# Two of the first weight loads of a recurrence-and-maxout kernel issued on the ScalarE queue instead of the SyncE queue

## The chip, the cores and the metric

The kernel runs on one core of a Trainium2 chip. The metric is the device time of one execution in microseconds.

The profile's span is counted from the first to the last instruction and is about 1.8 us shorter than the time of the same run.

## The reference, cut to what matters

```python
sig = 1 / (1 + exp(-f_logit));  f = lb + (1 - lb) * sig;  i = 1 - f
for t in range(S):                       # S = 6144, 4 sequences, 256 channels
    h = f[:, t] * h + i[:, t] * x[:, t]
    y[:, t] = h
h1 = y @ w1;  h2 = y @ w2                # 24576 tokens, 256 -> 1024
out = maximum(h1, h2) @ w_out            # 1024 -> 256
```

The kernel uses max(h1, h2) = h1 + relu(h2 - h1). It needs the difference w2 - w1, scaled and rounded to bf16 (`wd`), and the product w1 @ w_out (`w13` in the code, not to be confused with the load of the same name).

## The kernel before

The tokens are worked on in 48 blocks of 512. The weights and the first four blocks come in by 26 loads, nearly all of 256 KB, all on the SyncE queue and in this order:

```python
LOADS = """
f0a x0a f0b w13 w23 x0b w12 w22 wo3 w10 w20 w11 wo2 w21 f1a x1a wo0 f1b x1b wo1
f2a f2b x2a x2b f3 x3
"""
```

Here `f0a` is the first half of block 0 of `f_logit`, `x0b` the second half of block 0 of `x`, `w13` quarter 3 of w1, `w23` quarter 3 of w2, `wo3` quarter 3 of w_out. The names appear in the profile without their numbers: `fn`, `xn`, `w1n`, `w2n`, `won`.

A list says in which order each engine gets the small steps of the start. Its beginning:

```python
PLAN = """
G0a RW3.p keeps_T keeps V0a TU0a D31.p warm3 TV0a D30.p G0b F0a0.v warm4 TU0b
D21.p F0a1.v S0a1 S0a0 V0b F0b1.a warm1 TW3 F0b0.a RW0.p warm5 TV0b RW2.v S0b1
D01.p KW3.a TW2 SC31.a SC30.a KW2.a S0b0 RO3.a H06a H07a D20.v SC21.a warm3 H06b
SC20.v H07b D00.v W133 RW1.v R07.a TW0 H04b H04a ...
"""
```

The letter behind the point is the engine: v VectorE, a ScalarE, p GpSimd.
- `G` is the gate, a sigmoid of `f` on ScalarE; `V` is gate times `x` on VectorE (`vn` in the profile); `TU`, `TV` turn them on TensorE; `F` and `S` are the decay and the scan, with `y` as the result.
- `RW2` rounds quarter 2 of w1 (`w1b`); `D21`, `D20` subtract w1 from w2 (`wdf`), one half of a quarter each; `SC` scales the difference (`wd`).
- `H06b` and the like are the hidden matmuls `dT<-y,wd`; `warm` are matmuls that only keep TensorE busy. **H04b** is the ninth hidden matmul. From it on TensorE runs with hardly a gap, so its start is used below as the end of the start-up.

From block 4 on the tokens come another way. GpSimd issues a DMA that casts them to bf16 in DRAM (`cast`), and SyncE issues DMA transposes (`fT`, `xT`). The first cast waits for `x2b`, by a one-column copy into `held`.

```python
def load(j, s, half=None):
    ...
    nc.sync.dma_start(out=ins[j][s][:, q0:q1, :], in_=...)
...
nc.scalar.dma_start(out=lbr[:], ...)      # the lower bound, 1 KB
for name in LOADS.split():
    load_item(name)
```

Of the kernel before, what the change touches and what calls it, by code (L numbers as in the profile page):

```python
# [16 lines left out]
def kernel(  # L17
# [13 lines left out]
    nc = tc.nc  # L31
# [50 lines left out]
    w13 = wpool.tile([P, KC, D], BF16)  # L82
# [4 lines left out]
    def alloc_in(j):  # L87
        fn = inpool.tile([P, NQ, D], FP32, name="fn")
        xn = inpool.tile([P, NQ, D], FP32, name="xn")
        ins[j] = (fn, xn)  # L90
        us[j] = natpool.tile([P, NQ, D], BF16, name="un")
        vs[j] = natpool.tile([P, NQ, D], BF16, name="vn")
        ffs[j] = nffpool.tile([P, KC, TB], BF16, name="nff")
        ys[j] = ypool.tile([P, KC, TB], BF16, name="y")

    def load(j, s, half=None):

        src = (f_logit, x)[s]
        q0, q1 = (0, NQ) if half is None else (2 * half, 2 * half + 2)
        nc.sync.dma_start(  # L100
            out=ins[j][s][:, q0:q1, :],
            in_=src[0, j * TB + q0 * P : j * TB + q1 * P, :].rearrange(
                "(q p) d -> p q d", p=P
            ),
        )
# [70 lines left out]
    def turn_dma(c):  # L176
        for s, name in enumerate(("fs", "xs")):
            t = ttpool.tile([P, KC, CB * TB], BF16, name=("fT", "xT")[s])
            turned[c, s] = t
            nc.sync.dma_start_transpose(out=t[:], in_=spare[c % NS, name][:])  # L180

    def cast_behind(c):

        if c + 1 < NCH:
            last = CB * TB - 1
            nc.gpsimd.tensor_copy(out=held[:], in_=turned[c, 0][:, KC - 1, last : last + 1])  # L186
            cast(c + 1)
# [5 lines left out]
    def gate(j):  # L193
        ffs[j] = midpool.tile([P, KC, TB], BF16, name="ff")
        ys[j] = ypool.tile([P, KC, TB], BF16, name="y")
        us[j] = midpool.tile([P, KC, TB], BF16, name="u")
        nc.scalar.activation(out=us[j][:], in_=part(j, 0), func=AF.Sigmoid, scale=-1.0)  # L197

    def drive(j):
        vs[j] = midpool.tile([P, KC, TB], BF16, name="v")  # L200
        nc.vector.tensor_tensor(out=vs[j][:], in0=us[j][:], in1=part(j, 1), op=ALU.mult)  # L201

    def forget_half(j, h, on_act=False):
        forget(ffs[j][:, h, :], us[j][:, h, :], h, on_act)

    def scan_half(j, h):
        scan(j, h, 0, TB, vs[j][:, h, :])
# [45 lines left out]
    def hidden(j, fc):  # L253
        hidden_whole(j, fc)
        relu(j, fc)
# [49 lines left out]
    def project(j, slot):  # L305
        i, half_ = divmod(slot, 2)
        n = FC + KC
        project_steps(j, i, half_ * n // 2, (half_ + 1) * n // 2)
# [17 lines left out]
    def store(j, g):  # L326
        copy_out(j, g)
        send_out(j, g)

    def store_row(j, g, r):  # L330
        osb = lastpool.tile([P, D], FP32, name="row")
        nc.vector.tensor_copy(out=osb[:], in_=pos[j, g, r][:, 0, :])  # L332
        r0 = j * TB + 2 * g * P
        nc.sync.dma_start(
            out=out[r0 : r0 + 2 * P, :].rearrange("(p r) d -> p r d", r=2)[:, r, :],
            in_=osb[:],
        )
# [1 line left out]

    QF = DFF // 4  # L340

    def weight_load(k, w, src):
        cols = slice(k * QF, (k + 1) * QF)
        nc.sync.dma_start(  # L344
            out=w[:, :, cols], in_=src[:, cols].rearrange("(h p) f -> p h f", p=P)
        )

    def wout_load(k):
        nc.sync.dma_start(
            out=won[:, 2 * k : 2 * k + 2, :],  # L350
            in_=moe_w_out[k * QF : (k + 1) * QF, :].rearrange("(q p) c -> p q c", p=P),
        )
# [78 lines left out]
    def keep_warm(n):  # L431
        for _ in range(n):
            nc.tensor.matmul(  # L433
                idle[:].rearrange("p r d -> p (r d)"),
                lhsT=warm[:, 0:P],
                rhs=warm[:],
                start=True,
                stop=True,
            )
# [26 lines left out]

    engines = {"a": nc.scalar, "v": nc.vector, "p": nc.gpsimd}

    def load_item(name):
        if name[:2] == "wo":  # L470
            wout_load(int(name[2]))
        elif name[0] == "w":
            w, src = ((w1n, moe_w1), (w2n, moe_w2))[int(name[1]) - 1]
            weight_load(int(name[2]), w, src)
        else:
            half = ("ab".index(name[2]),) if len(name) == 3 else ()
            load(int(name[1]), "fx".index(name[0]), *half)

    outs = []

# [70 lines left out]
    with tc.manual_schedule():  # L551
        for j in range(NP):
            alloc_in(j)
        nc.scalar.dma_start(out=lbr[:], in_=lower_bound.rearrange("(h p) -> h p", p=P))
        for name in LOADS.split():
            load_item(name)
        nc.vector.memset(warm[:], 0.0)  # L557
        make_identity(nc, ident[:])
        nc.vector.tensor_copy(out=ident_b[:], in_=ident[:])
        keep_warm(7)  # L560
        for item in PLAN.split():
            issue(item)
        assert not outs

        for j in range(3, NBLK + 1):
            for fc in range(FC):
                if j < NBLK:
                    hidden(j, fc)
                project(j - 1, fc)
                if fc == 0 and j > 3:  # L570
                    store(j - 2, 1)
                if fc == 4 and j < NBLK:
                    store(j - 1, 0)
                if j == NBLK and fc in (3, 5, 7):
                    if fc == 3:
                        store(j - 1, 0)
                    else:
                        store_row(j - 1, 1, (fc - 5) // 2)
                if (j, fc) in gate_of:
                    b = gate_of[j, fc]  # L580
                    gate(b)
                    drive(b)
                    for h in range(KC):
                        forget_half(b, h)
                        scan_half(b, h)
                if (j, fc) in turn_of:
                    turn_dma(turn_of[j, fc])
                    cast_behind(turn_of[j, fc])
# [30 lines left out]
```

## Time and profile before

| | kernel before |
|---|---|
| median of 3 runs | 397.38 us (397.21 to 397.8) |
| TensorE busy | 387.6 of 395.6 us |
| DMA that the start waits for last, by the chain | x0b, issued 3.29, landed 8.71 us |
| H04b starts | 13.45 us |

First the page of the kernel before: span, busy time with its share and the number of instructions, and the chain that ended last, by engine.

```profile
span 395.6 us, 7146 instructions
## 1 busy us (share of the span) xinstructions
PE 387.6 (98%) x2793; PEld 275.0 (70%) x2840; DVE 251.2 (63%) x366; ACT 273.3 (69%) x451; POOL 39.2 (10%) x83
...
## 4 chain that ended last, share of the span: by engine, by line
PE 95%; DMA 1%; DVE 1%; issue 1%; SPq 1%; DVEq 0%
...
```

TensorE is busy nearly everywhere, and it makes 95% of the chain. What is left is the start. The stages of one microsecond show it; the columns are as the head line says, and the last two are the mean share of the 16 DMA engines (it can pass 1 where packets overlap) and what they moved.

```profile
...
core 0: us, PE busy (x) PEld busy (x) DVE busy (x) ACT busy (x) POOL busy (x), PEclk, DMA share, GB/s
2.00:3.00 1.00, 1.00 (x4) 0.43 (x3) 0.00 (x0) 0.60 (x1) 0.00 (x0) 1.00 0.86 241
3.00:4.00 1.00, 1.00 (x4) 0.18 (x2) 0.00 (x0) 0.38 (x1) 0.00 (x0) 1.00 0.99 327
4.00:5.00 1.00, 1.00 (x7) 0.70 (x7) 0.41 (x3) 0.25 (x1) 0.00 (x0) 1.00 0.88 296
5.00:6.00 1.00, 1.00 (x4) 0.34 (x3) 0.94 (x3) 0.00 (x0) 0.00 (x0) 1.00 1.04 331
6.00:7.00 1.00, 1.00 (x8) 0.52 (x7) 0.42 (x1) 0.63 (x1) 0.14 (x1) 1.00 0.83 284
9.00:10.00 1.00, 0.15 (x1) 0.00 (x0) 1.00 (x2) 0.90 (x2) 0.46 (x1) 1.00 1.06 361
...
```

From 9 us on the loads come at about 350 GB/s, before that a little slower. Then the timeline of VectorE from x0b's landing (start, duration, engine, line, operation, names; in brackets the idle time before it and what ended that):

```profile
...
start us, us, engine line op out<-in xcount [idle before <-releaser]
8.80 1.20 DVE L113 TENSOR_TENSOR vn<-un,xn 128x512 bf16<-128x512 bf16 x1 [0.96 <-DMA xn<-in_x_dram]
9.93 0.41 DVE L355 CAST w1b<-w1n 128x512 bf16<-128x512 f32 x1
10.56 1.38 DVE L149 TENSOR_TENSOR_SCAN y<-nff,y,dT 128x256 bf16<-128x256 bf16 x2 [0.21 <-issue]
11.86 0.79 DVE L380 TENSOR_TENSOR wdf<-w2n,w1n 128x256 f32<-128x256 f32 x1
12.68 0.72 DVE L388 TENSOR_SCALAR wd<-wdf,om 128x256 bf16<-128x256 f32 x1
...
```

and of TensorE, GpSimd and ScalarE in the same stretch:

```profile
...
10.06 0.40 PE L126 MATMUL dT<-ident_b,vn 128*128 128x128 bf16 x4 [0.91 <-DVE vn L113]
...
13.45 0.72 PE L225 MATMUL dT<-y,wd 128*128 128x256 bf16 x5 [0.20 <-DVE wd L388]
```

```profile
...
8.05 1.41 POOL L380 TENSOR_TENSOR wdf<-w2n,w1n 128x256 f32<-128x256 f32 x2 [0.58 <-DMA w2n<-in_moe_w_dram]
...
```

```profile
...
1.32 1.28 ACT L108 ACT_TABLE_LOAD   x1 [1.32 <-PEq L603]
3.62 0.63 ACT L108 ACTIVATE un<-fn 128x512 bf16<-128x512 f32 x1 [1.02 <-DMA fn<-in_f_logit_dram]
6.11 0.63 ACT L108 ACTIVATE un<-fn 128x512 bf16<-128x512 f32 x1 [1.86 <-DMA fn<-in_f_logit_dram]
...
```

VectorE works without a real pause from 8.80 to 13.40, and TensorE's matmul at 13.45 has waited 0.20 us for its last `wd`. In the chain of waits this reads as "x0b, then VectorE, then TensorE". The `vn` at 8.80 took 1.20 us; the one at 4.73 took 0.68, as most do.

### The profile page before, as it was taken

To read this page: it belongs to the slowest core of one execution; us is meant where nothing else is said; L and a number is where in the kernel's file an instruction comes from. 1 tells how busy PE (TensorE), PEld (TensorE's weight loads), DVE (VectorE), ACT (ScalarE), POOL (GpSimd) and SP (SyncE) were. 2 spreads that over 40 slices of the span, in tenths; PEclk is the share of its full clock that TensorE was granted. 3 is DMA by queue.
4 is the path that set the end of the run, shared out by engine and by line. 5 is a ranking of instruction groups with operands and counts; after the bars stand their busy time and mean duration, and the time that the engine had idled before them with its cause. 6 is when DMAs were issued, how large, how long until landed. Compare 5 with 4: busy or idle time off the path is not lost.

```text
span 395.6 us, 7146 instructions
## 1 busy us (share of the span) xinstructions
PE 387.6 (98%) x2793; PEld 275.0 (70%) x2840; DVE 251.2 (63%) x366; ACT 273.3 (69%) x451; POOL 39.2 (10%) x83
## 2 busy tenths in 40 slices
PE   8999999999999999999999999999999999999996
PEld 3796777676667777767677777666677777676775
DVE  4896965756755775576567656755775576567622
ACT  4787676677667666766676677667766766676661
POOL 2511011011101101001011011011011010100000
PEclk9999999999999999999999999999999999999999
DMA  7989999999999999999999999999898898981122
GB/s 252 350 220 211 211 206 216 216 221 225 200 228 201 203 230 178 229 220 202 199 232 209 188 228 191 195 208 230 198 204 213 186 202 193 217 188 55 53 81 107
DMA packets 125078, 79.12 MB, mean 200 GB/s; under 512 B 94194, under 2 KB 101620, under 8 KB 125044
## 3 DMA queue, kind: packets, MB, share of 16 engines
q1 hardware_dynamic: 113072, 55.59, 59.8%
q0 software_dynamic: 11968, 23.07, 35.7%
q8 instruction: 22, 0.36, 0.4%
q14 instruction: 12, 0.10, 0.1%
q10 hardware_dynamic: 4, 0.00, 0.0%
HBM read 53.48 MB, written 48.23 MB: 257 GB/s over the span
## 4 chain that ended last, share of the span: by engine, by line
PE 95%; DMA 1%; DVE 1%; issue 1%; SPq 1%; DVEq 0%
PE psO L268 53%; PE dT L245 39%; PE dT L225 2%; DMA xn<-in_x_dram 1%; PE dT L126 1%; SPq L100 0%; PE psO L413 0%; DVE vn L113 0%; SPq L344 0%; DVE y L149 0%; DVE wd L388 0%; DVE wdf L380 0%; DVE row L332 0%; PE dT L396 0%; DVEq L113 0%
## 5 line engine op out<-in xcount | busy, mean ns | idle before, releaser
L240 ACT ACTIVATE rt<-dT 128x512 bf16<-128x512 f32 x382 | 222.9, 596 | 104.4 <-PE dT L245 101.2
L268 PE MATMUL psO<-wob,rt 128*128 128x256 bf16 x1536 | 231.0, 273 | 0.2
L268 PEld LDWEIGHTS <-rt 128*128 128x128 bf16 x1536 | 150.0, 98 | 94.7 <-issue 0.2
L245 PE MATMUL dT<-y,wd 128*128 128x512 bf16 x690 | 208.8, 379 | 2.2
L149 DVE TENSOR_TENSOR_SCAN y<-ff,y,v 128x512 bf16<-128x512 bf16 x82 | 105.2, 1283 | 2.9
L317 DVE COPY osb<-psO 128x512 f32<-128x512 f32 x93 | 62.6, 678 | 65.6 <-PE psO L268 65.6
L245 PEld LDWEIGHTS <-wd 128*128 128x128 bf16 x736 | 72.0, 98 | 8.8
L268 PE MATMUL psO<-w,y 128*128 128x256 bf16 x384 | 72.4, 273 | 0.0
L201 DVE TENSOR_TENSOR v<-u,xT 128x1024 bf16<-128x1024 bf16 x44 | 30.4, 691 | 62.7 <-ACT u L197 50.8
L197 ACT ACTIVATE u<-fT 128x1024 bf16<-128x1024 bf16 x44 | 46.1, 1049 | 3.1 <-DMA fT<-fs 3.1
L268 PEld LDWEIGHTS <-y 128*128 128x128 bf16 x384 | 37.6, 98 | 4.4
L186 POOL CAST held<-fT 128x1 f32<-128x1 bf16 x21 | 6.7, 319 | 278.9 <-DMA fT<-fs 278.9
L138 DVE TENSOR_SCALAR ff<-u,nom 128x512 bf16<-128x512 bf16 x88 | 29.7, 338 | 0.0
L170 POOL DMA_DIRECT2D fs<-in_f_logit_dram x22 | 12.3, 558 | 4.3 <-issue 4.3
L170 POOL DMA_DIRECT2D xs<-in_x_dram x22 | 12.1, 549 | 0.0
L149 DVE TENSOR_TENSOR_SCAN y<-nff,y,dT 128x256 bf16<-128x256 bf16 x14 | 9.6, 731 | 1.8 <-PE dT L126 1.5
L225 PE MATMUL dT<-y,wd 128*128 128x256 bf16 x64 | 10.1, 273 | 0.3 <-DVE wd L388 0.2
L433 PE MATMUL psO<-warm 128*128 128x512 bf16 x22 | 7.8, 492 | 1.2 <-DVE warm L557 1.2
L149 DVE TENSOR_TENSOR_SCAN y<-ff,v 128x512 bf16<-128x512 bf16 x6 | 7.4, 1225 | 0.2
L108 ACT ACTIVATE un<-fn 128x512 bf16<-128x512 f32 x8 | 5.0, 628 | 3.3 <-DMA fn<-in_f_logit_dram 3.0
L225 PEld LDWEIGHTS <-wd 128*128 128x128 bf16 x64 | 5.8, 98 | 1.4 <-issue 0.4
L113 DVE TENSOR_TENSOR vn<-un,xn 128x512 bf16<-128x512 bf16 x8 | 6.1, 767 | 1.0 <-DMA xn<-in_x_dram 1.0
(40 smaller groups left out, 52.2 us busy)
## 6 DMA issues: line engine op xcount, KB each, us to landing
out_dram<-osb SPq DMA_DIRECT2D x95, 256.0 KB, 3.4
fs<-in_f_logit_dram POOLq DMA_DIRECT2D x22, 512.0 KB, 6.8
xs<-in_x_dram POOLq DMA_DIRECT2D x22, 512.0 KB, 9.6
fn<-in_f_logit_dram SPq DMA_DIRECT2D x6, 256.0 KB, 6.0
xn<-in_x_dram SPq DMA_DIRECT2D x6, 256.0 KB, 5.7
w1n<-in_moe_w_dram SPq DMA_DIRECT2D x4, 256.0 KB, 5.9
w2n<-in_moe_w_dram SPq DMA_DIRECT2D x4, 256.0 KB, 6.0
won<-in_moe_w_out_dram SPq DMA_DIRECT2D x4, 256.0 KB, 6.0
```

The source lines that it names most:

```text
L138: nc.vector.tensor_scalar(out=o, in0=i, scalar1=nom[:, h : h + 1], scalar2=1.0, op0=ALU.mult, op1=ALU.add)
L149: nc.vector.tensor_tensor_scan(out=ys[j][:, h, t0:t1], data0=ffs[j][:, h, t0:t1], data1=v, initial=initial, op0=ALU.mult, op1=ALU.add,)
L170: nc.gpsimd.dma_start(out=spare[c % NS, name][:], in_=src[b, k * TB : (k + CB) * TB, :], max_dma_last_dim=4096,)
L186: nc.gpsimd.tensor_copy(out=held[:], in_=turned[c, 0][:, KC - 1, last : last + 1])
L197: nc.scalar.activation(out=us[j][:], in_=part(j, 0), func=AF.Sigmoid, scale=-1.0)
L201: nc.vector.tensor_tensor(out=vs[j][:], in0=us[j][:], in1=part(j, 1), op=ALU.mult)
L225: nc.tensor.matmul(dts[j, fc][:, tok], lhsT=wd[:, kc, unit(fc)], rhs=ys[j][:, kc, tok], start=(first and kc == 0), stop=(not first and kc ...
L240: nc.scalar.activation(out=rt[:], in_=dts[j, fc][:], func=AF.Relu)
L245: nc.tensor.matmul(dts[j, fc][:], lhsT=wd[:, kc, unit(fc)], rhs=ys[j][:, kc, :], start=(kc == 0), stop=(kc == KC - 1),)
L268: nc.tensor.matmul(ps, lhsT=lhsT, rhs=rhs, start=start, stop=stop, skip_group_check=True)
L317: nc.vector.tensor_copy(out=osbs[j, g][:], in_=pos[j, g, 0][:])
L433: nc.tensor.matmul(idle[:].rearrange("p r d -> p (r d)"), lhsT=warm[:, 0:P], rhs=warm[:], start=True, stop=True,)
```

## The change

The intent: SyncE needs 0.51 us for each issue, so the sixth load goes out only at 3.29. ScalarE has a queue too, and until its first gate at 3.62 it only issues one small load and loads a table (1.32 to 2.60). Two weight loads are issued there, beside the token loads.

```diff
-    def load(j, s, half=None):
+    def load(j, s, half=None, eng=nc.sync):
...
-    def weight_load(k, w, src):
+    def weight_load(k, w, src, eng=nc.sync):
         cols = slice(k * QF, (k + 1) * QF)
-        nc.sync.dma_start(
+        eng.dma_start(
...
         for name in LOADS.split():
-            load_item(name)
+            load_item(name, nc.scalar if name in ("w13", "w23") else nc.sync)
```

More of the change, by code (lines that the diff above doesn't have):

```diff
@@ L340 @@
     QF = DFF // 4
-    def weight_load(k, w, src):
+    def weight_load(k, w, src, eng=nc.sync):
         cols = slice(k * QF, (k + 1) * QF)
-        nc.sync.dma_start(
+        eng.dma_start(
             out=w[:, :, cols], in_=src[:, cols].rearrange("(h p) f -> p h f", p=P)
@@ L467, with load_item @@
     engines = {"a": nc.scalar, "v": nc.vector, "p": nc.gpsimd}
-    def load_item(name):
+    def load_item(name, eng=nc.sync):
         if name[:2] == "wo":
@@ L473, in load_item @@
             w, src = ((w1n, moe_w1), (w2n, moe_w2))[int(name[1]) - 1]
-            weight_load(int(name[2]), w, src)
+            weight_load(int(name[2]), w, src, eng)
         else:
             half = ("ab".index(name[2]),) if len(name) == 3 else ()
-            load(int(name[1]), "fx".index(name[0]), *half)
+            load(int(name[1]), "fx".index(name[0]), *half, eng=eng)
     outs = []
```

## The prediction

> **What bounds the kernel now.** TensorE. The page has it busy for 387.6 of 395.6 us at full clock, and PE is 95% of the chain that ended last. In the table of stages TensorE is fully busy from 14 to 380 us (278.2 of the 280 us from 100 to 380). So the change can only shorten the start, the first 13.45 us, and shift the rest by as much.
>
> **The start, from the timeline and the chain of waits.** In 0 to 30 us the chain runs through the SyncE issues, then the DMA of x0b (issued at 3.29, landed after 5.42 us, at 8.71), then VectorE without a pause: vn (8.80, 1.20 us), y, wdf, wd, to TensorE at 13.45. Before that TensorE runs mostly warm-up matmuls; after it, it does not pause.
> SyncE takes 0.51 us per 256 KB issue; landings in the steady stretch come every 0.73 to 0.75 us (350 GB/s in the stages from 9 to 23 us). So the transfers, not the issues, limit the loads from about 3 us on. Only the stages 2 to 7 us are under that rate (241, 327, 296, 331, 284 GB/s).
>
> **What the change does.** Two issues (w13, w23) leave SyncE; ScalarE gets them after its own small load (0.73 to 1.28): at about 1.3 and 1.8 us instead of 2.27 and 2.78. SyncE's later issues come 1.0 us earlier. ScalarE's table load (1.28 us, now at 1.32) starts about 1.0 us later and ends at about 3.6, just when the first gate can start now (3.62): no loss there, or a few tenths.
> The Trainium skill, "DMA: Bandwidth & Descriptors", section "Issuing engines are not separate DMA queues", says that the queues share the same 16 DMA engines and only issue time is saved; the 0.73 us per landing in this trace agrees. So I expect:
> 1. f0a lands a little later (3.6 to about 3.9), x0a later by 0.4 to 0.9 us (4.3 to about 5), f0b about unchanged (6.1): they now share the engines with the weights. Mostly hidden: VectorE now idles from 7.9 to 8.8.
> 2. w13 lands at about 5.2 instead of 6.8, w23 at about 6.2 instead of 8.0. The subtractions on GpSimd then end at about 8 instead of 9.46.
> 3. x0b is still the last of the same six transfers. It gains only what the fuller start of the DMA engines gains: from the bytes missing at 2 to 7 us, estimated at most 0.75 us; I take 0.3.
> 4. The vn at 8.80 takes 1.20 us beside GpSimd's subtractions, against a median of 0.68. The Trainium skill, "SBUF — State Buffer", section "Who interferes with whom", says that a VectorE instruction with two SBUF inputs contends with a GpSimd instruction that reads SBUF. With GpSimd done earlier this vn should take about 0.7 us: 0.5 us saved on the chain.
> 5. Against that, the following landings (w12, w22, w10, w20: 9.4 to 12.5) move by only about 0.3 us and hold back part of it.
>
> Sum: TensorE's first unbroken stretch starts at about 12.9 instead of 13.45, and all of it reaches the end: about 396.8 us against 397.38, 0.15% less.
>
> **Range and chances.** 395.9 to 397.9 us. Faster by over 2%: 0.5%; within 2%: 98.5%; slower by over 2%: 1%.
>
> **What would show it.** Landings of w13 and w23 at least 1 us earlier; the vn after x0b near 0.7 us; x0b landing 8.2 to 8.6; the same TensorE busy time; the steady 0.73 us per landing.
>
> **What would make it wrong.** The late token loads could delay the first scans past x0b, or the table load past f0a, and turn the gain into a loss of up to 0.5 us; or the weight landings after x0b could hold the start where it is.

## The result, and the profile after

| | before | after | ratio |
|---|---|---|---|
| first result | 397.38 us (397.21 to 397.8, 4 runs) | 397.08 us (396.21 to 397.54, 4 runs) | 0.9988 [0.9969, 1.0007] |
| same kernel again (e1) | 397.36 us (9 runs) | 396.83 us (5 runs) | 0.9982 [0.9969, 0.9995] |
| and again (e9) | 397.54 us (11 runs) | 396.90 us (6 runs) | 0.9998 [0.9979, 1.0017] |

A ratio is the mean time of one kernel's fast runs over that of the other's of the same rounds, so it isn't quite the ratio of the medians. The bracket is its 95% interval.

The time is the same within 2%, and a small gain is likely but not clear of noise: of the three intervals only that of e1 ends below 1. The means of all runs differ by 0.47, 0.81 and 0.17 us, while the kernel before, run against itself (e2), differed from its own runs by 0.36 us (397.19 against 397.55, means).

The page after, the same lines:

```profile
span 395.8 us, 7193 instructions
...
PE 389.9 (99%) x2840; PEld 274.9 (69%) x2840; DVE 251.5 (64%) x366; ACT 273.5 (69%) x451; POOL 39.1 (10%) x83
...
PE 96%; DMA 2%; ACT 1%; SPq 0%; DVE 0%; issue 0%
...
```

The span of this profiled run is 395.8, against 395.6 before: this execution shows no gain at all (its time, 397.54, was the slowest of the four). TensorE's busy time differs by 2.3 us, but so does the count of matmul records (2,793 and 2,840 for 2,840 weight loads in both), so that is missing records, not work. The chain has changed: its DMA is now `fn` (f0b), and ScalarE has taken VectorE's place in it. The stages:

```profile
...
2.00:3.00 1.00, 1.00 (x4) 0.43 (x3) 0.00 (x0) 0.69 (x1) 0.00 (x0) 1.00 0.85 243
3.00:4.00 1.00, 1.00 (x4) 0.17 (x2) 0.00 (x0) 0.99 (x2) 0.00 (x0) 1.00 0.96 320
4.00:5.00 1.00, 1.00 (x7) 0.70 (x7) 0.23 (x2) 0.24 (x1) 0.00 (x0) 1.00 0.90 263
5.00:6.00 1.00, 1.00 (x4) 0.18 (x2) 0.00 (x0) 0.00 (x0) 0.00 (x0) 1.00 1.05 304
6.00:7.00 1.00, 0.13 (x1) 0.00 (x0) 0.31 (x1) 0.00 (x0) 0.14 (x1) 1.00 1.00 325
9.00:10.00 1.00, 1.00 (x12) 0.65 (x10) 1.00 (x3) 0.76 (x3) 1.00 (x2) 1.00 1.09 351
...
```

The bytes come no faster: from 2 to 7 us 1,455 KB after (243 + 320 + 263 + 304 + 325) against 1,479 KB before (241 + 327 + 296 + 331 + 284). The rate from 9 us on is about 350 GB/s in both. ScalarE:

```profile
...
1.32 0.42 ACTq L344 DMA_DIRECT2D w1n<-in_moe_w_dram  x1
1.77 0.51 ACTq L344 DMA_DIRECT2D w2n<-in_moe_w_dram  x1
2.31 1.28 ACT L108 ACT_TABLE_LOAD   x1 [2.31 <-issue]
3.61 0.63 ACT L108 ACTIVATE un<-fn 128x512 bf16<-128x512 f32 x1
8.12 0.63 ACT L108 ACTIVATE un<-fn 128x512 bf16<-128x512 f32 x1 [3.88 <-DMA fn<-in_f_logit_dram]
...
```

The two issues delayed the table load by 1.0 us to 2.31, and it ended just as f0a landed: the first gate starts at 3.61 (3.62 before), so ScalarE's time was free. But the second gate now waits for f0b until 8.12 instead of 6.11. GpSimd, VectorE and TensorE:

```profile
...
8.70 2.72 POOL L380 TENSOR_TENSOR wdf<-w2n,w1n 128x256 f32<-128x256 f32 x3 [0.84 <-DMA w2n<-in_moe_w_dram]
...
```

```profile
...
9.19 0.78 DVE L113 TENSOR_TENSOR vn<-un,xn 128x512 bf16<-128x512 bf16 x1
9.89 0.94 DVE L355 CAST w1b<-w1n 128x512 bf16<-128x512 f32 x1
11.04 1.39 DVE L149 TENSOR_TENSOR_SCAN y<-nff,y,dT 128x256 bf16<-128x256 bf16 x2 [0.20 <-ACT wd L390]
12.34 0.52 DVE L380 TENSOR_TENSOR wdf<-w2n,w1n 128x256 f32<-128x256 f32 x1
...
```

```profile
...
7.44 0.40 PE L126 MATMUL dT<-ident_b,vn 128*128 128x128 bf16 x4 [1.31 <-DVE vn L113]
...
13.67 0.50 PE L225 MATMUL dT<-y,wd 128*128 128x256 bf16 x3
```

H04b now has no idle time before it. The chain of waits that leads to it no longer begins with x0b, but with f0b (start, duration, what; cut to four steps):

```profile
...
1.76 6.34 DMA fn<-in_f_logit_dram
8.12 0.64 ACT un L108
...
10.55 0.81 ACT wd L390 x2
11.41 0.61 PE dT L225 x4
...
```

From f0b's landing it runs through the gate, TensorE, ScalarE's own list of steps up to `wd`, and then TensorE's list, three warm-up matmuls (0.65 us) among them, to H04b. The chains of e1 and e9 are the same.

Where the 16 semaphore steps of each load fall in the trace tells when each load had landed (us; the last step counts):

```
             before   e2 (before)   after    e1 (after)   e9 (after)
f0a           3.60       3.57        3.48       3.57         3.67
x0a           4.30       4.27        6.59       5.05         5.02
f0b           6.09       5.93        8.10       7.91         7.31
w13           6.80       7.11        6.81       5.43         5.96
w23           7.98       7.84        8.62       8.10         7.52
x0b           8.71       8.58        8.94       8.71         8.22
w12           9.44       9.33        9.71       9.47         8.98
H04b starts  13.45      13.34       13.67      13.48        13.00
```

The tokens x0a and f0b land 0.7 to 2.3 us later, in all three profiles. Their place in the engines was taken by w13 and w23, which nevertheless gained little: w13 0 to 1.7 us, w23 between 0.8 us too late and 0.5 us early. The rest of the loads stands where it stood.

Two things fit this. First, the queues share the engines: the Trainium skill, "DMA: Bandwidth & Descriptors", section "Queues, rings and completion order", says that each DMA engine serves its queues in turn, packet by packet, and the landings agree. Second, a load has landed when the slowest of 16 engines is done, and these drift apart. In the profile before, 13 of the 16 steps of f0b came between 4.81 and 5.12, the other three at 5.98, 6.02 and 6.09. After, 15 steps of x0a came between 4.03 and 4.77 and the last at 6.59. In this load nearly all data was there almost two microseconds before it counted as landed.

### The profile page after: what moved, and what is told of

It reads as the page before. It is cut to its first block, busy times and chain, and to the rows that moved or that the text cites. A ratio compares the mean times of both kernels' runs of the same rounds, so it can differ in the third digit from the quotient of the medians.

```text
span 395.8 us, 7193 instructions
## 1 busy us (share of the span) xinstructions
PE 389.9 (99%) x2840; PEld 274.9 (69%) x2840; DVE 251.5 (64%) x366; ACT 273.5 (69%) x451; POOL 39.1 (10%) x83
## 4 chain that ended last, share of the span: by engine, by line
PE 96%; DMA 2%; ACT 1%; SPq 0%; DVE 0%; issue 0%
PE psO L268 53%; PE dT L245 40%; PE dT L225 2%; DMA fn<-in_f_logit_dram 2%; PE dT L126 1%; PE psO L413 0%; SPq L100 0%; ACT nff L134 0%; ACT wd L390 0%; PE psO L433 0%; ACT un L108 0%; ACT w1T L355 0%; PE dT L396 0%; DVE row L332 0%
## 5 line engine op out<-in xcount | busy, mean ns | idle before, releaser
L245 PE MATMUL dT<-y,wd 128*128 128x512 bf16 x736 | 218.6, 379 | 0.0
L149 DVE TENSOR_TENSOR_SCAN y<-ff,y,v 128x512 bf16<-128x512 bf16 x82 | 105.2, 1283 | 2.9
L186 POOL CAST held<-fT 128x1 f32<-128x1 bf16 x21 | 5.9, 282 | 280.4 <-DMA fT<-fs 280.4
L225 PE MATMUL dT<-y,wd 128*128 128x256 bf16 x64 | 10.1, 273 | 0.1
```

What stands on the lines that cost most here:

```text
L149: nc.vector.tensor_tensor_scan(out=ys[j][:, h, t0:t1], data0=ffs[j][:, h, t0:t1], data1=v, initial=initial, op0=ALU.mult, op1=ALU.add,)
L186: nc.gpsimd.tensor_copy(out=held[:], in_=turned[c, 0][:, KC - 1, last : last + 1])
L225: nc.tensor.matmul(dts[j, fc][:, tok], lhsT=wd[:, kc, unit(fc)], rhs=ys[j][:, kc, tok], start=(first and kc == 0), stop=(not first and kc ...
L245: nc.tensor.matmul(dts[j, fc][:], lhsT=wd[:, kc, unit(fc)], rhs=ys[j][:, kc, :], start=(kc == 0), stop=(kc == KC - 1),)
```

## The experiments

Three theories were kept apart. The first is the prediction's: x0b's landing and the VectorE work behind it hold the start, and less contention with GpSimd shortens that. Theory A says that two queues share the engines, so that the tokens land late. Theory T, formed after the first four runs, says that the start hangs on the whole train of landings (one load every 0.75 us), so that moving single loads within it gains nothing.

### The changed kernel again, and the kernel before against itself

The kernels are unchanged.

> The changed kernel once more, with more rounds and a second profile. If the small gain of the first result is real, the ratio to the kernel before is about 0.9985 with an interval below 1; if it is run-to-run spread, the ratio is 0.9995 to 1.0005. In the new profile, theory A (two queues share the DMA engines, so the second and third token loads land late) wants x0a at 6 us or later and f0b at about 8 us again; the rival that the first profile caught a hiccup wants them near 5.0 and 6.3.

> The kernel before against itself: ratio 1.000, and its interval shows what spread the others have to beat; I expect single runs to differ by up to 0.6 us. The second profile shows whether the late third landing (f0b 1.8 us after x0a) comes again: theory of a random stall of one DMA engine says it moves or vanishes, theory of a fixed cause says 6.1 us again.

e1 measured 396.83 us, ratio 0.9982 [0.9969, 0.9995]. f0b was late again (7.91), and so was its gate; x0a came at 5.05, so the 6.59 of the first profile was partly a hiccup of one engine. That each half of the expectation fits one load is a mixed answer: the late f0b belongs to the change, the very late x0a doesn't always come.

e2 measured 397.21 us, ratio 0.9993 [0.998, 1.0005]. The late f0b of the kernel before came again, at 5.93, but with the steps spread evenly, not by three stragglers. So the loss of rate at 4 to 6 us is usual and which engines lose it changes.

### The order of the loads alone

```diff
 e3:  -f0a x0a f0b w13 w23 x0b      +f0a x0a w13 f0b w23 x0b
 e4:  -f0a x0a f0b w13 w23 x0b      +f0a x0a f0b x0b w13 w23
```

> All loads on the SyncE queue, but in the order in which the changed kernel's landings came (w13 before f0b). If only the order of the loads matters, f0b lands at about 8 us as in the changed kernel and the time is that of the changed kernel. If the sharing of the engines between two queues is what delays the tokens (theory A), x0a lands at 4.3 us as before, w13 at about 5.5, f0b at about 6.8, and the time is within 0.2 us of the kernel before, since x0b stays sixth.

> All on the SyncE queue, x0b moved ahead of w13 and w23. If x0b is what the start waits for (the chain of the kernel before), x0b lands at about 7 us instead of 8.7 and the unbroken TensorE stretch starts up to 0.7 us earlier, total about 396.7 us. If the weights hold the start as much as x0b does, the time is the same or up to 0.5 us longer, because w23 is then sixth and GpSimd ends its subtractions later.

e3, on one queue, gave x0a at 4.20, w13 at 6.85 and f0b at 7.58. The late x0a of the changed kernel therefore belongs to the second queue, as theory A has it. (The line is not quite sharp: e10 below, on one queue, had x0a at 4.95, its last step 0.61 us behind the fifteenth. The other five profiles with one queue have 4.20 to 4.30, the eight with two 4.93 to 6.59.) The late f0b comes from the order alone in good part: 7.58 lies between the two expectations, nearer to that of the order. The time was 397.69 us by the median, ratio 0.9999 [0.9986, 1.0012], no difference to the kernel before.

e4 is the telling one. x0b landed at 6.62 instead of 8.71, over two microseconds earlier, and the time was 397.17 us, ratio 0.9998 [0.9984, 1.0011]. VectorE in e4:

```profile
...
7.39 0.67 DVE L113 TENSOR_TENSOR vn<-un,xn 128x512 bf16<-128x512 bf16 x1
9.33 0.99 DVE L355 CAST w1b<-w1n 128x512 bf16<-128x512 f32 x1 [1.27 <-DMA w1n<-in_moe_w_dram]
10.38 1.39 DVE L149 TENSOR_TENSOR_SCAN y<-nff,y,dT 128x256 bf16<-128x256 bf16 x2
...
```

`vn` now takes 0.67 us, as the prediction wished, and is done at 8.06 instead of 10.00. Then VectorE sits idle 1.27 us until w12 has landed (9.30), and the cast takes 0.99 us instead of 0.41, because GpSimd now works beside the cast. H04b starts at 13.31 instead of 13.45. So taking away the wait for x0b and the 1.20 us `vn` gained almost nothing: the next wait, for w12, stood right behind it.

Over the profiles of all kernels with the same steps a simple rule comes out. H04b starts at a fixed time after w12 landed:

```
          w12 landed   H04b starts   difference
before       9.44         13.45         4.01
e2           9.33         13.34         4.01
after        9.71         13.67         3.96
e1           9.47         13.48         4.01
e9           8.98         13.00         4.02
e3           9.82         13.84         4.02
e4           9.30         13.31         4.01
e5           8.93         12.93         4.00
e6          10.03         14.03         4.00
```

w12 is only the first of those that count: the following loads (w22, wo3, w10) come at fixed steps of 0.75 us behind it, so the rule can't tell which of them holds.

The rule is a regularity, not a cause, for the chains of waits that lead to H04b differ. In before, e2 and e5 the chain comes from x0b and `vn`, in e4 from w12 and its cast; in e3 and the three profiles of the changed kernel it comes from f0b. In the changed kernel H04b started 5.57, 5.57 and 5.69 us after f0b had landed, which is as regular as 4.0 us after w12. VectorE ended its last `wd` before H04b only 0.05 to 0.06 us earlier there, so both paths end nearly together; but VectorE's second scans had waited 0.20, 0.48 and 0.35 us before, by the trace for ScalarE's `wd`, a step of f0b's chain. (e6's chain does not pass through H04b.)

### Half the change, and the issue slots kept

e5 gives only w13 to ScalarE. e6 is the changed kernel with two 1 KB loads on SyncE where w13 and w23 were.

```diff
 e5:  -... if name in ("w13", "w23") else nc.sync
      +... if name == "w13" else nc.sync
 e6:  +if name in ("w13", "w23"):
      +    nc.sync.dma_start(out=tiny[name == "w23"][:], in_=lower_bound...)
```

> Half of the change: only w13 goes to the ScalarE queue. In the six profiles so far the first H04b matmul (where TensorE's unbroken stretch begins) started 3.96 to 4.02 us after w12 landed, whatever the order of the loads (theory T: the start hangs on the train of landings). T expects that again, and a total that moves with the landing of w12: between 396.8 and 397.4 us. If the gain of the changed kernel comes from the freed issue time of SyncE, half of it (0.3 us) stays.

> The changed kernel, but SyncE issues two 1 KB loads in the places where w13 and w23 were, so its other issues come no earlier than in the kernel before. If the gain of 0.1 to 0.2% comes from the issue time that SyncE saves, it is gone: ratio 0.9995 to 1.0005. If it comes from the second queue itself, the ratio stays near 0.9985. Theory T expects w12 to land at 9.3 to 9.7 us, and the first H04b matmul 4.0 us after.

e5: 396.82 us, ratio 0.9992 [0.9979, 1.0005]; H04b 4.00 us after w12, as theory T has it. With one weight load on the second queue f0b landed at 6.76 (7.31 to 8.10 with two), the chain to H04b no longer began with it, and H04b came at 12.93. The size of the gain can't be told from none or from that of the full change.

e6: 398.10 us, ratio 1.0022 [1.0009, 1.0035], slower than expected by all theories, and not a clean test. Its profile is of the slowest of six runs (399.53; the others took 397.56 to 398.41). In it SyncE stood still for over 3 us before it issued w22, until w13 had landed (7.08). The loads take turns on eight semaphores in the trace, and the two tiny loads moved this wait forward from w10 (issued at 6.83 in the first profile after the change, right after w13's landing at 6.81) to w22. So they cost more than their issue time. w12 landed at 10.03, where theory T expected 9.3 to 9.7, and H04b followed at 14.03. What follows is only the rule again; whether saved issue time matters stays open.

### One more load, and twice the change

e7 adds a useless 256 KB load to the kernel before, between x0b and w12. e8 puts w13, w23, w12 and w22 on the ScalarE queue.

```diff
 e7:  -... w23 x0b w12 w22 ...            +... w23 x0b extra w12 w22 ...
 e8:  -name in ("w13", "w23")             +name in ("w13", "w23", "w12", "w22")
```

> The kernel before with one useless 256 KB load between x0b and w12. If x0b and the VectorE chain after it hold the start, as the prediction had it, x0b still lands at 8.6 us, w12 0.75 us later, and only part of that shows: about 0.3 us longer. Theory T expects all of it: w12 lands at about 10.1, the first H04b matmul at 14.1, the total 0.7 to 0.8 us longer (about 398.1 us, ratio 1.0019).

> Twice the change: w13, w23, w12 and w22 on the ScalarE queue. ScalarE's table load starts 0.9 us later than in the changed kernel (about 3.2) and ends at about 4.5, so the first gate starts at 4.5 instead of 3.6. If the second queue speeds up the whole train of landings, w22 lands at 9.5 us or earlier and the total is below 396.6 us. If the queues only share the same engines (theory T), the tokens land later still, w22 at about 10.1, and the total is 397.0 to 397.8 us.

e7: 398.76 us, ratio 1.0038 [1.0025, 1.0051], about 1.5 us longer. That is twice what theory T expected and five times what the prediction's chain would give. But the six runs fall in two groups: 398.10 to 398.32, where T put it, and 399.21 to 399.73. The profile is of the slowest. In it H04b starts at 14.16, 0.71 us later than before, and later TensorE waits 0.73 us at 22.25 for the rounding of wo1, whose load also came late. So in this execution the train of loads held TensorE twice, at H04b and again eight microseconds later. Not all of that need be the extra load's doing: x0b, before which nothing was changed, landed at 9.46 instead of 8.71 (and w12 at 10.94, not 10.1), and from wo1 on the last step of every load came about 2.0 us after the fifteenth, so that one of the 16 engines had fallen behind. H04b came only 3.22 us after w12 here. x0b no longer stood directly before w12, and the matmuls before H04b waited for the weights of w10 instead; the rule of 4.0 us is one of this order of loads.

e8: 398.07 us, ratio 1.0017 [1.0002, 1.0033], slower than expected. Three runs took 396.95 to 397.44, three 398.71 to 398.96, and the profile (398.78) is of the second group; why there are two is not known. ScalarE paid for its issues:

```profile
...
3.35 1.28 ACT L108 ACT_TABLE_LOAD   x1 [3.35 <-issue]
4.64 0.63 ACT L108 ACTIVATE un<-fn 128x512 bf16<-128x512 f32 x1
...
```

The first gate started 1.0 us later than before (3.62), w22 landed at 10.19 as theory T had it, w12 at 8.98. H04b came at 14.19, and VectorE's second pair of scans before it had waited 1.41 us for ScalarE's `wd`; so here ScalarE's late work came before the train as a limit. By the mean of its runs, two more loads on this queue were a loss.

### A third repeat, and one step moved off VectorE

e9 is the changed kernel. e10, e11 and e12 move D20, one subtraction, from VectorE to a gap of GpSimd: in the kernel before, in the changed one, and in e5.

```diff
-D21.p F0a1.v ...  H06a H07a D20.v SC21.a ...
+D21.p D20.p F0a1.v ...  H06a H07a SC21.a ...
```

> The changed kernel a third time, to settle whether its gain is real. The first two results gave 0.9988 and 0.9982. If the gain is real, the ratio is 0.998 to 0.9992 again; if it was chance, 0.9995 or more. In the profile, theory T expects the first H04b matmul 4.0 us after w12 landed (if w12 landed between 8.8 and 10 us), and a landing of w12 that lies where the kernel before has it, 9.3 to 9.8 us, since the queues share the engines.

> The kernel before with one subtraction (the second half of w22 - w12, called D20) moved from VectorE to the gap of GpSimd behind D21. If the VectorE work between w12's landing and H04b holds the start (as the chain of waits says), the step D20 of 0.5 to 0.8 us leaves that chain, and the first H04b matmul starts 3.5 to 3.8 us after w12 instead of 4.0: total 0.2 to 0.5 us shorter, ratio about 0.999. If the landings of w10 and wo3 hold it (train alone), nothing is gained.

> The same move of D20 in the changed kernel. If the two gains are independent, the ratio is about 0.9975 to 0.998 (396.4 us). If the changed kernel had its gain from the same stretch of VectorE work (less contention with GpSimd, as the prediction had it), the move adds nothing: 0.9985.

> Only w13 on the ScalarE queue, and D20 moved to GpSimd. If w13 alone is as good as both loads, this is as fast as the kernel with both and D20 moved, within 0.2 us; the first H04b matmul comes 3.5 to 3.8 us after w12.

| | median | ratio to before | w12 to H04b |
|---|---|---|---|
| e9 | 396.90 us | 0.9998 [0.9979, 1.0017] | 4.02 us |
| e10 | 397.43 us | 0.9997 [0.9983, 1.001] | 3.44 us |
| e11 | 396.74 us | 0.9984 [0.997, 0.9998] | 3.88 us |
| e12 | 396.64 us | 0.9982 [0.9966, 0.9997] | 3.64 us |

e9's ratio says "chance" by its own expectation, and w12 landed earlier (8.98) than theory T had it (9.3 to 9.8). Four of its six runs lie between 396.63 and 396.91, the others at 397.80 and 398.74; why is not known, for those two have no profile.

By the expectation written before e10, its 3.44 us say that VectorE's work behind w12 is on the path, and that the landings of w10 and wo3 alone don't hold H04b. e12 agrees (3.64), and its time is within 0.2 us of e11's, as expected. In e11 the same move bought only about 0.1 us (3.88): f0b landed at 7.97, the chain began with it as in the changed kernel, and H04b came 5.50 us after it. So with both weights on the second queue, the late f0b holds the start about as much as VectorE's work does.

e10 shows something new. H04b came 0.24 us earlier (13.21 against 13.45), and 0.57 us of the work behind w12 was gone, yet the span was 396.1, not shorter. The loss is far from the start. This is ScalarE and then TensorE of e10 around 66 to 69 us:

```profile
...
66.22 1.06 ACT L197 ACTIVATE u<-fT 128x1024 bf16<-128x1024 bf16 x1 [2.85 <-DMA fT<-fs]
...
```

```profile
...
69.28 0.28 PE L268 MATMUL psO<-wob,rt 128*128 128x256 bf16 x1 [0.20 <-ACT rt L240]
...
```

ScalarE's gate for a later block waited 2.85 us for the transposed tokens `fT`. The `relu` steps behind it came late, and TensorE lost 0.8 us around here (the stretch from the 121st to the 161st weight load of the hidden matmuls took 20.37 us instead of 19.55; only part of it is shown as a gap). The same gate before and after the change:

```profile
...
65.67 1.06 ACT L197 ACTIVATE u<-fT 128x1024 bf16<-128x1024 bf16 x1 [2.04 <-DMA fT<-fs]
...
```

```profile
...
64.62 1.06 ACT L197 ACTIVATE u<-fT 128x1024 bf16<-128x1024 bf16 x1 [0.78 <-DMA fT<-fs]
...
```

All 14 profiles fit one picture. Where this wait was 1.1 us or less, TensorE lost nothing here. At 2.04 us (before) it lost 0.07, at 2.10 (e12) 0.06, at 2.24 (e2) 0.38, at 2.85 (e10) 0.82 us. Apart from this stretch and the start the kernels are alike: from the 161st of these weight loads to the last took 311.93 us in every profile.

The wait seems to hang on the end of the train of loads; this was not tested by itself. The first cast starts when x2b has landed:

```profile
...
23.74 0.42 POOL L537 COPY held<-xn 128x1 f32<-128x1 f32 x1 [3.83 <-DMA xn<-in_x_dram]
...
```

```profile
...
22.54 0.19 POOL L537 COPY held<-xn 128x1 f32<-128x1 f32 x1 [2.43 <-DMA xn<-in_x_dram]
...
```

x2b landed at 23.7, 23.4 and 23.3 us in three profiles with one queue (before, e2, e10), and at 22.5, 22.7 and 22.4 in those of the changed kernel (after, e1, e9). The one-queue kernels e3 (22.9) and e4 (23.3) lie between and at the upper end, and lost nothing, so one queue doesn't force the loss; it comes closer to it. The other profiles with these 26 loads agree: x2b landed at 22.5 (e5), 21.7 (e8), 22.7 (e11) and 22.5 (e12), so that seven profiles with a second queue have 21.7 to 22.7 and five with one queue 22.9 to 23.7. But x2b isn't all: e12's gate waited 2.10 us, and its H04b was the earliest of all (12.28).

e11 and e12 are the fastest kernels, with intervals that end below 1. They are not told apart from the changed kernel, whose ratio in the same rounds was 0.9998 [0.9979, 1.0017], an interval that covers theirs in good part. So no clear winner can be named.

## Why the prediction was right or wrong

The time: 397.08 us lies inside 395.9 to 397.9, close to the forecast of 396.8, and "same within 2%" is right. But the forecast gain of about 0.6 us is hardly larger than the spread, and the way to it was largely wrong, so that the forecast came so close is in good part luck. Point by point:

- **TensorE is the limit and passes every shift of the start on.** Right, with one exception. From H04b on everything took the same time, but the stretch around 65 us can swallow or give back up to 0.8 us. (In e6, e7 and e8, with other or later loads, another 0.4 to 1.0 us was lost before: H04b to the 121st weight load took 42.4 to 43.0 us instead of 42.0.) The prediction said that all of a shorter start reaches the end; e10 shows a start that came 0.24 us earlier and a time that did not fall.
- **Step 1, "f0a lands a little later, x0a later by 0.4 to 0.9 us, f0b about unchanged".** f0a was unchanged. x0a was later by 0.7 to 2.3 us, f0b by 1.2 to 2.2. This step failed. "Mostly hidden" failed too: f0b's gate became part of the chain.
- **Step 2, "w13 lands at about 5.2, w23 at about 6.2, subtractions end at about 8".** w13 landed at 6.81, 5.43 and 5.96, w23 at 8.62, 8.10 and 7.52. GpSimd's two subtractions ended at 10.55, 10.08 and 9.01, where the forecast was 8 and the kernel before had 9.46. This step failed: being issued 1.0 us earlier on another queue bought w23 nothing clear.
- **Step 3, x0b 0.3 us earlier.** It landed at 8.94, 8.71 and 8.22 against 8.71 and 8.58: no clear change, and the bytes of the stages from 2 to 7 us did not grow.
- **Step 4, "this vn should take about 0.7 us: 0.5 us saved on the chain".** The duration came true in two of three profiles (0.78, 0.69, then 1.24), but by luck, and the saving never came. In those two GpSimd was not done earlier, as the step has it: its second subtraction still ran beside `vn` (9.39 to 10.55, and 8.87 to 10.08), and this time it was GpSimd's step that took longer, 1.16 and 1.21 us instead of 0.72. The next step, the cast of w12, then took 0.94 and 0.88 us instead of 0.41. Together the two took 1.61 us before and 1.72, 1.57 and 1.65 after. The contention moved from one step to the next. The Trainium skill, "SBUF — State Buffer", section "Who interferes with whom", names a VectorE step with two inputs in SBUF as one that contends with GpSimd's reads, and a cast as one that can contend; the durations here agree. The prediction applied it to one step only.
- **Step 5, "hold back part of it".** This was the mis-sized term: all of it was held back. e4 took away the wait for x0b and gained almost nothing, because w12 came next. In the changed kernel it was the late f0b of step 1 from which the chain ran. The prediction had named both as dangers ("late token loads", "the weight landings after x0b") and given them too little weight. H04b stayed at w12 plus 4.0 us in nine profiles.
- **"TensorE's first unbroken stretch starts at about 12.9".** Measured 13.67, 13.48 and 13.00, on average 13.38, against 13.45 and 13.34 before. In the profiles the start has gained nothing.
- **The table load past f0a**, named as a danger, did not happen with two issues (3.61), and did with four (4.64 in e8).

Where a gain would come from, if it is real, was seen but not tested by itself: the end of the train of loads is about a microsecond earlier with two queues, the first cast follows it, and the later gate waits 0 to 0.8 us instead of 2.0 to 2.2, so that TensorE doesn't lose the 0.07 to 0.38 us that it lost in the two profiles of the kernel before. That is less than the mean differences of 0.47 and 0.81 us. In the first result and in e1 the profiled execution was the slowest of its set, so the profiles may not show all of the gain. Why the train ends earlier stays open. In the profiles before and e2 one landing near 21 us came 2.2 us after the one before it instead of 0.75, soon after a 16 KB instruction load that starts near 19 us; after the change the largest step between the 256 KB loads there was 0.8, 1.2 and 1.5 us. That is three profiles each way, not a cause. The steps show more: in before, from f2a on, the last step of each load came about 1.5 us after the fifteenth, and in e2 1.3 to 1.4 us. So one of the 16 engines had fallen behind and made every later landing late. The same is seen in e4 (1.3 to 1.4), e12 (1.1), e5 and e10 (0.8), so it isn't tied to one queue. Every profile has one such instruction load, 1.1 us long, in the first 21 us; whether the engine that fell behind is the one that carried it can't be read from the traces kept.

## What to carry to other kernels

Where loads already come near the full rate of the DMA engines, a second queue may only change who goes first: here it was paid for by the token loads that the first queue carried. Before shortening the wait that the chain names, ask what stands right behind it: here the next load, 0.75 us later, was just as much a limit, and a kernel that takes the first wait away (e4) shows it at once. Then read the chain of the changed kernel anew; here it ran from another load, f0b. An earlier start may be lost again where a later stage waits for its own stream of loads (e10).

## What the Trainium skill lacked or had wrong

- "DMA: Bandwidth & Descriptors", "Issuing engines are not separate DMA queues": it says that issuing on several engines only saves issue time. The runs agree that the bytes come no faster (1,455 against 1,479 KB from 2 to 7 us), but the section lacks the price: loads issued at about the same time on the other queue land later (x0a 0.7 to 2.3 us, f0b 1.2 to 2.2 us), and the issuing engine pays 0.4 to 0.5 us for each (first gate 1.0 us later with four issues in e8).
- The same page explains the 16 steps of a load's semaphore, but no page says how far the engines drift apart: the last of 16 came up to 1.8 us after the fifteenth (x0a in the profile after), and in the profiles before, e2, e4 and e7 the last of 16 stayed 1.3 to 2.0 us behind for the rest of the train. A landing says little about when most of the data was there.
- "SBUF — State Buffer", "Who interferes with whom": right for the instructions here (`vn` 0.68 or 1.20 us, the cast 0.41 or 0.94 us). It lacks a warning that shifting such steps can move the contention to the next step or to GpSimd's own (1.61 us before, 1.57 to 1.72 us after for the pair; GpSimd's subtraction 0.72 or 1.16 us).
- "ScalarE: Activation LUTs", "What ACT_TABLE_LOAD costs": its 1283 ns for the load agree with 1.28 us in the traces. The drain of about 1.38 us that it adds for every switch to a different set doesn't show at this first load of the program: the gate started 0.02 us after the end of the load (2.31 + 1.28, gate at 3.61).
